# Two pieces of an output projection in the other order: 256 columns ahead of 384

## The chip, the cores and the metric

The kernel runs on one core of one Trainium2 chip. The metric is the device time of one execution in microseconds (us). Three runs of the kernel before took 623.13, 623.89 and 624.4 us. About 0.2%, some 1.25 us, is what a measurement of this kernel can tell from no change.

## The reference, cut to what matters

```python
def _A_ref(x, wqkv, wo):                     # x: 1 x 2048 x 640, H = 32 heads of 20
    qkv = (x @ wqkv).reshape(B, S, 3, H, Dh)...
    # each position attends to W = 8 positions, 2 apart, itself the first
    logits = einsum("bhsd,bhswd->bhsw", q, kg) * scale
    attn = softmax(where(mask, logits, -1e9))
    o = einsum("bhsw,bhswd->bhsd", attn, vg)
    return o.reshape(B, S, D) @ wo

def _B_ref(x, w1, w2):                       # w1: 640 x 1536, w2: 1536 x 640
    return silu(x @ w1) @ w2

xn = layernorm(x)
return x + _A_ref(xn, A_wqkv, A_wo) * silu(_B_ref(xn, B_w1, B_w2))
```

The change concerns the product with `wo`, the output projection of the attention, 640 columns wide.

## The kernel before, in words

The 2048 tokens are worked on in four groups of 512, a group being four tiles (`t`) of 128 tokens. All matrix products are done with 32-bit operands that are split into a high and a low part; a product is the sum of three: high x high, high x low and low x high. The stationary operand of a matmul has 128 x 128 elements, and each matmul has a weight load of its own, also when the stationary operand is the one that is loaded already.

For each group the matmul engine (PE) does, in this order: QKV in four quarters (lines 726 to 760, the matmuls are lines 745 to 747; the first three quarters have 512 columns, the fourth 384); the output projection of the group before (`wo_phase`, lines 796 to 821; not in the first group); and the feed-forward network, FFN, in six stages (`ffn_phase`, lines 877 to 944). A stage of the FFN is two times 15 matmuls of 512 columns (`up`, lines 890 to 892) and then 24 pairs of the kind below (`down`). After the last group comes the output projection of that group (`wo_last`, lines 823 to 875). So three output projections stand between a QKV and an FFN, and a fourth at the end.

The projection and the second product of the FFN have 640 result columns for a token tile, and a PSUM bank holds 512 values. So each product is done as a pair (`tm_mm`, line 770): a 384-column matmul (`CA`, line 774) into a bank of its own for each token tile (`a[t]`), and a 256-column one (`CB`, line 776) into a bank that two token tiles share (`b[t // 2]`). In `wo_phase` the loop runs over the five chunks `c` of 128 of the 640 rows of `wo`. For each chunk the four tiles come one after the other with the high part of the attention's result (`OH`), first times the high, then times the low part of the weights (`big`, four matmuls); then the four tiles with the low part (`OL`) times the high part of the weights (`small`, two matmuls). That is 5 x (4 x 2 + 4) = 60 pairs in a phase, 180 in the three phases. `OH` and `OL` lie in the same tiles (`thl`) that hold the transposed input of QKV, 16 columns further on.

The order of the work is set by a planner (`Weave`, line 63): each step is put on record with its engine, an estimated duration and the buffers that it reads and writes; the steps of PE keep the order in which they are recorded, and those of the other engines are placed by a list scheduler. The matmuls inside `big` or `small` are one step, so their order is that in which the function issues them.

Around `wo_phase`: QKV's last quarter leaves its results in four banks, which ScalarE copies out (lines 533 and 536); these become the four wide banks `a`. The narrow banks `b` are taken first (`tm_banks(True)`) and are two banks of the third quarter. When the projection is finished, VectorE multiplies it by the gate (line 813), the four wide banks first and then the two narrow ones. The FFN writes these banks again in its first `down`, after two `up` steps. The weights come through a ring of seven slots (`w`), filled by DMAs on GpSimd's queue (line 410) as slots are given back (`w_done`).

Of the kernel before, what the change touches and what calls it, by code (L numbers as in the profile page):

```python
# [18 lines left out]
DC, FC = D // P, F // P  # L19
# [35 lines left out]
def tsl(t):  # L55
    return slice(t * P, (t + 1) * P)
# [6 lines left out]
class Weave:  # L63
# [22 lines left out]
    def add(self, eng, dur, fn, reads=(), writes=(), prio=0.0, lock=False, table=None, nbytes=0, late=0.0):  # L86
        o = Op()
        o.late = late
        o.eng, o.dur, o.fn, o.prio, o.lock, o.table, o.nbytes = eng, dur, fn, prio, lock, table, nbytes
        o.seq, o.users, o.ready = len(self.ops), [], 0.0  # L90
        before = set()
        for k in reads:
            if k in self.writer:
                before.add(self.writer[k])
        for k in writes:
            if k in self.writer:
                before.add(self.writer[k])
            before.update(self.readers.get(k, ()))
        for k in writes:
            self.writer[k] = o  # L100
            self.readers[k] = []
        for k in reads:
            self.readers.setdefault(k, []).append(o)
        before.discard(o)
        o.left = len(before)
        for b in before:
            b.users.append(o)
        self.ops.append(o)
        return o
# [104 lines left out]
def local_attention_silu_ffn(ctx: ExitStack, tc: tile.TileContext, x, wqkv, wo, w1, w2, out):  # L214
# [14 lines left out]
    def rows(view, g):  # L229
        h, par = groups[g]  # L230
        return view[h, :, par::2, :]
# [20 lines left out]
    def turned_tiles(half, shift):  # L252
        n = DC * TOK
        return [t[:, half * n + shift:(half + 1) * n + shift].rearrange("p (c m) -> p c m", c=DC) for t in THL]
    TH, TL = turned_tiles(0, 0), turned_tiles(1, 0)
    OH, OL = turned_tiles(0, SHIFT), turned_tiles(1, SHIFT)
# [20 lines left out]
    def take(kind, n):  # L277
        i = count[kind] % n
        count[kind] += 1
        return i  # L280
# [15 lines left out]
    def dve(n, fn, reads, writes, prio, lock=False):  # L296
        add("DVE", dv(n), fn, reads, writes, prio, lock)
# [4 lines left out]
    def pe(dur, fn, reads, writes):  # L302
        add("PE", dur, fn, reads, writes)
        clock[0] += dur

    def dma(fn, reads, writes, nbytes, prio, dur=0.45, late=0.0):
        add("SP", dur, fn, reads, writes, prio, nbytes=nbytes, late=late)
# [125 lines left out]
    def w_next(*want):  # L433

        i = used[0]
        assert units[i] == want and i < loaded[0], (units[i], want)
        used[0] += 1
        s, n = i % RING, width(want)
        return WR[s][:, :n], WR[s][:, n:2 * n], ("wh", s), ("wl", s)

    def w_done(n=1):
        for _ in range(n):
            w_load()
# [318 lines left out]
    def t_keys(i, cs, ts=range(T), kinds=("th", "tl")):  # L762
        return [(k, i, c, t) for k in kinds for c in cs for t in ts]

    def tm_banks(narrow_first=False):
        b = [bank() for t in range(T // 2)] if narrow_first else None
        a = [bank() for t in range(T)]
        return a, b or [bank() for t in range(T // 2)]

    def tm_mm(banks, t, st, w, first, last, cols=(0, 1)):  # L770
        a, b = banks
        h = t % 2
        if 0 in cols:
            nc.tensor.matmul(a[t][0][:, :CA], st, w[:, :CA], start=first, stop=last)  # L774
        if 1 in cols:
            nc.tensor.matmul(b[t // 2][0][:, h * CB:(h + 1) * CB], st, w[:, CA:], start=first and h == 0,  # L776
                             stop=last, skip_group_check=True)

    def tm_views(banks, order="aaaabb"):

        a, b = banks
        n = {"a": 0, "b": 0}
        for kind in order:
            k = n[kind]
            n[kind] += 1
            if kind == "a":
                yield a[k][0][:, :CA].rearrange("p (t m) -> p t m", t=1), a[k][1], slice(k, k + 1), slice(0, CA)
            else:
                yield b[k][0].rearrange("p (t m) -> p t m", t=2), b[k][1], slice(2 * k, 2 * k + 2), slice(CA, D)

    def gkeys(ts, cs):
        return [("g", t, cs.start) for t in range(ts.start, ts.stop)]
# [3 lines left out]
    def wo_phase(g, i):  # L796
        banks = tm_banks(True)
        a, b = banks
        for c in range(DC):
            wh, wl, kh, kl = w_next("wo", c)  # L800
            for t in range(T):
                def big(c=c, t=t, wh=wh, wl=wl):
                    tm_mm(banks, t, OH[i][:, c, tsl(t)], wh, c == 0, False)
                    tm_mm(banks, t, OH[i][:, c, tsl(t)], wl, False, False)
                pe(2 * TM, big, t_keys(i, [c], [t], ["th"]) + [kh, kl], [a[t][1], b[t // 2][1]])
            for t in range(T):
                def small(c=c, t=t, wh=wh):
                    tm_mm(banks, t, OL[i][:, c, tsl(t)], wh, False, c == DC - 1)
                pe(TM, small, t_keys(i, [c], [t], ["tl"]) + [kh], [a[t][1], b[t // 2][1]])
            w_done()  # L810
        for p, kp, ts, cs in tm_views(banks):
            n = (ts.stop - ts.start) * (cs.stop - cs.start)
            dve(n, lambda p=p, ts=ts, cs=cs: nc.vector.tensor_tensor(
                out=G[:, ts, cs], in0=p, in1=G[:, ts, cs], op=OP.mult), [kp], gkeys(ts, cs), 0)
        for t in range(T):
            s = take("xr", 2)
            xr = XR[s]
            dma(lambda t=t, xr=xr: nc.sync.dma_start(xr, rows(xg, g)[:, t, :]), [], [("xr", s)], P * D * 4, clock[0] + 5)
            add("POOL", po(D), lambda t=t, xr=xr: nc.gpsimd.tensor_tensor(out=xr, in0=xr, in1=G[:, t, :], op=OP.add),
                [("g", t, 0), ("g", t, CA)], [("xr", s)], 500, lock=True)  # L820
            dma(lambda t=t, xr=xr: nc.sync.dma_start(rows(og, g)[:, t, :], xr), [("xr", s)], [], P * D * 4, clock[0] + 20)
# [165 lines left out]
```

## Time and profile before

| | |
|---|---|
| median of three runs | 623.89 us (623.13 to 624.4) |
| the profiled execution | 621.75 us, its span 620.0 us |
| instructions | 9090 |
| PE: matmuls | 3357, busy 614.5 us |
| three output projections between QKV and FFN | from 195.06, 346.88 and 498.56 us, 18.00, 18.00 and 17.99 us each |
| output projection at the end | from 598.95 us |
| DMA | 162.45 MB, mean 262 GB/s |

The time of an execution is longer than its span by 1.75 us, which lie around the first and the last instruction. In the views, PE is the matmul engine and PEld its weight loads, which overlap the matmuls. A matmul's duration in the trace is modelled and overlaps the next one's, so a matmul's cost is read from the distance between two starts. `L774` is line 774 of the kernel. In a row of the form `acc<-w,thl` the output stands left of the arrow (`acc` and `rot` are PSUM banks), the operands right of it. In the timeline the first number is the start in microseconds from the start of the span, the second the duration; what stands in brackets at the end of a row is the idle time of the engine before it and what ended that.

### The profile page before, as it was taken

What the parts mean: (1) busy time and instruction counts of PE and PEld (TensorE: products, weight loads), DVE (VectorE), ACT (ScalarE), POOL (GpSimd) and SP (SyncE); (2) the same over time, 40 slices, a digit from 0 to 9 for tenths busy, and PEclk for the clock granted to TensorE, in tenths of its full rate; (3) what the DMA queues carried; (4) which work ended last, traced back from release to release, by engine and by line L of the source; (5) the groups of instructions that cost most, each with busy time, mean ns of one, the idle gap of its engine ahead of it and who ended that gap; (6) DMA issues with size and microseconds to landing.
All of it is one profiled execution on the core that took longest, in us unless ns stands there. A gap on an engine that the chain in (4) does not pass through costs nothing.

```text
span 620.0 us, 9090 instructions
## 1 busy us (share of the span) xinstructions
PE 614.5 (99%) x3357; PEld 555.1 (90%) x3357; DVE 562.0 (91%) x581; ACT 309.5 (50%) x651; POOL 112.9 (18%) x168
## 2 busy tenths in 40 slices
PE   8999999999999999999999999999999999999997
PEld 7889899998889999999888999999988999999997
DVE  6458999999989998999999989999979999899974
ACT  5435558927476213951944502583396316153650
POOL 4510000001101133111212233311121213311100
PEclk9999999999999999999999999999999999999999
DMA  8999999876999998764799999855579999966642
GB/s 255 339 277 321 358 369 395 333 236 174 349 299 350 341 347 247 239 194 136 204 240 255 338 327 309 270 179 162 167 198 277 253 328 277 318 184 194 206 135 102
DMA packets 65449, 162.45 MB, mean 262 GB/s; under 512 B 7053, under 2 KB 29165, under 8 KB 65405
## 3 DMA queue, kind: packets, MB, share of 16 engines
q0 software_dynamic: 20016, 82.58, 44.5%
q1 hardware_dynamic: 45389, 79.29, 40.4%
q8 instruction: 26, 0.43, 0.3%
q14 instruction: 18, 0.15, 0.1%
HBM read 109.55 MB, written 34.16 MB: 232 GB/s over the span
## 4 chain that ended last, share of the span: by engine, by line
PE 97%; SPq 1%; DMA 1%; DVE 0%; issue 0%; ACT 0%
PE acc L774 22%; PE acc L776 15%; PE acc L747 10%; PE acc L746 10%; PE acc L745 10%; PE rot L892 9%; PE rot L891 9%; PE rot L890 9%; PE acc L684 1%; DMA xin<-in_A_x_dram 1%; PE rot L776 1%; SPq L384 0%; SPq L385 0%; PE rot L774 0%; PE acc L872 0%; PE rot L662 0%
## 5 line engine op out<-in xcount | busy, mean ns | idle before, releaser
L747 PE MATMUL acc<-w,thl 128*128 128x512 f32 (+1 forms) x300 | 112.5, 375 | 0.0
L746 PE MATMUL acc<-w,thl 128*128 128x512 f32 (+1 forms) x300 | 112.5, 375 | 0.0
L745 PE MATMUL acc<-w,thl 128*128 128x512 f32 (+1 forms) x300 | 112.5, 375 | 0.0
L774 PE MATMUL acc<-w,sh 128*128 128x384 f32 x384 | 111.6, 334 | 0.0
L776 PE MATMUL acc<-w,sh 128*128 128x256 f32 x384 | 107.3, 279 | 0.0
L896 ACT ACTIVATE sh<-rot 128x512 fp32r<-128x512 f32 x48 | 28.7, 597 | 155.4 <-PE rot L892 155.4
L892 PE MATMUL rot<-thl,w 128*128 128x512 f32 x240 | 93.9, 391 | 0.0
L891 PE MATMUL rot<-thl,w 128*128 128x512 f32 x240 | 93.8, 391 | 0.0
L890 PE MATMUL rot<-thl,w 128*128 128x512 f32 x240 | 93.6, 390 | 0.0
L579 DVE TENSOR_TENSOR pr<-q,kv 128x2560 f32<-128x2560 f32 x32 | 90.1, 2817 | 1.5 <-DMA raw<-in_A_wqkv_dram 1.3
L617 DVE TENSOR_TENSOR pr<-e,kv 128x2560 f32<-128x2560 f32 x32 | 90.3, 2822 | 0.7
L582 DVE TENSOR_REDUCE l<-pr 128x128 f32<-128x2560 f32 x32 | 90.0, 2813 | 0.5
L622 DVE TENSOR_TENSOR pr<-pr 128x1280 f32<-128x1280 f32 x64 | 74.0, 1156 | 1.5
L410 POOL DMA_DIRECT2D w<-half_w x72 | 38.5, 535 | 191.8 <-PE acc L776 98.5
L776 PEld LDWEIGHTS acc<-w,sh 128*128 128x128 f32 x384 | 72.3, 188 | 0.9
L774 PEld LDWEIGHTS acc<-w,sh 128*128 128x128 f32 x384 | 72.1, 188 | 1.1
L410 POOL DMA_DIRECT2D w<-half_q x52 | 27.6, 531 | 238.6 <-PE rot L892 107.2
L774 PE MATMUL acc<-w,thl 128*128 128x384 f32 x225 | 65.5, 341 | 0.0
L745 PEld LDWEIGHTS acc<-w,thl 128*128 128x128 f32 x300 | 56.3, 188 | 8.7
L746 PEld LDWEIGHTS acc<-w,thl 128*128 128x128 f32 x300 | 56.3, 188 | 8.7
L747 PEld LDWEIGHTS acc<-w,thl 128*128 128x128 f32 x300 | 56.3, 188 | 8.5
L495 ACT ACTIVATE xin<-sf 32x256 f32<-32x256 f32 (+1 forms) x144 | 54.6, 379 | 9.7 <-DVE sf L522 8.0
(92 smaller groups left out, 1044.7 us busy)
## 6 DMA issues: line engine op xcount, KB each, us to landing
w<-half_w POOLq DMA_DIRECT2D x72, 640.0 KB, 5.8
w<-half_q POOLq DMA_DIRECT2D x39, 512.0 KB, 4.5
half_w<-w SPq DMA_DIRECT2D x24, 640.0 KB
w<-half_wo POOLq DMA_DIRECT2D x15, 640.0 KB, 5.5
kv<-kv SPq DMA_DIRECT2D x15, 560.0 KB
half_q<-w SPq DMA_DIRECT2D x15, 512.0 KB
kv<-kv SPq DMA_DIRECT2D x15, 420.0 KB
gate<-in_B_w_dram SPq DMA_DIRECT2D x16, 320.0 KB
```

Of the source, the lines that this page charges most:

```text
L579: dve(2560, lambda t=t: nc.vector.tensor_tensor(out=PR, in0=win(qq[:, t:t + 2, :], W, 0), in1=win(kv[:, 0, t:t + 2, :], W, CQ), op=OP.mult ...
L582: dve(2560, lambda t=t: nc.vector.tensor_reduce(out=l[:, t:t + 2].rearrange("p t w h -> p (t w h)"), in_=PR.rearrange("p t w (h d) -> p (t ...
L617: dve(2560, lambda t=t, v=v: nc.vector.tensor_tensor(out=PR.rearrange("p t w (h d) -> p t (w h) d", d=DH), in0=e[:, t:t + 2].rearrange("p ...
L622: dve(2 * k * CQ, lambda k=k: nc.vector.tensor_tensor(out=PR[:, :, 0:k, :], in0=PR[:, :, 0:k, :], in1=PR[:, :, k:2 * k, :], op=OP.add), [] ...
L745: nc.tensor.matmul(o, hi, wh, start=c == 0, stop=False)
L746: nc.tensor.matmul(o, lo, wh, start=False, stop=False)
L747: nc.tensor.matmul(o, hi, wl, start=False, stop=c == DC - 1)
L774: nc.tensor.matmul(a[t][0][:, :CA], st, w[:, :CA], start=first, stop=last)
L776: nc.tensor.matmul(b[t // 2][0][:, h * CB:(h + 1) * CB], st, w[:, CA:], start=first and h == 0, stop=last, skip_group_check=True)
L890: nc.tensor.matmul(h, wh[:, cs], TH[i][:, c, :], start=c == 0, stop=False)
L891: nc.tensor.matmul(h, wh[:, cs], TL[i][:, c, :], start=False, stop=False)
L892: nc.tensor.matmul(h, wl[:, cs], TH[i][:, c, :], start=False, stop=c == DC - 1)
```

## The change

In `wo_phase` alone the 256-column matmul of each pair is issued ahead of the 384-column one. `tm_mm` is rewritten so that the argument `cols` gives the order, not only the choice; FFN and `wo_last` keep calling it with the wide one first. The estimated durations of the steps stay, and so does the planner's order on every engine.

```diff
     def tm_mm(banks, t, st, w, first, last, cols=(0, 1)):
         a, b = banks
         h = t % 2
-        if 0 in cols:
+        def wide():
             nc.tensor.matmul(a[t][0][:, :CA], st, w[:, :CA], start=first, stop=last)
-        if 1 in cols:
+
+        def narrow():
             nc.tensor.matmul(b[t // 2][0][:, h * CB:(h + 1) * CB], st, w[:, CA:], start=first and h == 0,
                              stop=last, skip_group_check=True)
+        for k in cols:
+            (wide, narrow)[k]()
...
                 def big(c=c, t=t, wh=wh, wl=wl):
-                    tm_mm(banks, t, OH[i][:, c, tsl(t)], wh, c == 0, False)
-                    tm_mm(banks, t, OH[i][:, c, tsl(t)], wl, False, False)
+                    tm_mm(banks, t, OH[i][:, c, tsl(t)], wh, c == 0, False, (1, 0))
+                    tm_mm(banks, t, OH[i][:, c, tsl(t)], wl, False, False, (1, 0))
...
                 def small(c=c, t=t, wh=wh):
-                    tm_mm(banks, t, OL[i][:, c, tsl(t)], wh, False, c == DC - 1)
+                    tm_mm(banks, t, OL[i][:, c, tsl(t)], wh, False, c == DC - 1, (1, 0))
```

On PE, the entry of the first output projection, with the last matmul of QKV ahead of it, before. `acc_109` and `acc_110` are wide banks, `acc_107` is the narrow bank of the tiles 0 and 1; behind a row stands the engine on whose work it waits.

```order
L747 MATMUL acc_106<-w_74,thl_71 128x384
L774 MATMUL acc_109<-w_75,thl_67 128x384 [waits Activation_49]
L776 MATMUL acc_107<-w_75,thl_67 128x256
L774 MATMUL acc_109<-w_75,thl_67 128x384 [waits DVE_49]
L776 MATMUL acc_107<-w_75,thl_67 128x256
L774 MATMUL acc_110<-w_75,thl_67 128x384 [waits Activation_49]
```

The same place after the change (the narrow matmul is now line 777):

```order
L747 MATMUL acc_106<-w_74,thl_71 128x384
L777 MATMUL acc_107<-w_75,thl_67 128x256 [waits Activation_49]
L774 MATMUL acc_109<-w_75,thl_67 128x384 [waits Activation_49]
L777 MATMUL acc_107<-w_75,thl_67 128x256 [waits DVE_49]
L774 MATMUL acc_109<-w_75,thl_67 128x384
L777 MATMUL acc_107<-w_75,thl_67 128x256
L774 MATMUL acc_110<-w_75,thl_67 128x384 [waits Activation_49]
```

The narrow matmul has moved up one place in each pair, and the waits for the operands have moved to it; the waits for the wide banks stay with the wide matmuls.

On PE, the end of the same phase and the first matmul of the FFN, before:

```order
L774 MATMUL acc_105<-w_79,thl_67 128x384
L776 MATMUL acc_108<-w_79,thl_67 128x256
L774 MATMUL acc_106<-w_79,thl_67 128x384
L776 MATMUL acc_108<-w_79,thl_67 128x256
L890 MATMUL rot_111<-thl_71,w_80 128x512 [waits DMASW4_49]
```

And after:

```order
L777 MATMUL acc_108<-w_79,thl_67 128x256
L774 MATMUL acc_105<-w_79,thl_67 128x384
L777 MATMUL acc_108<-w_79,thl_67 128x256
L774 MATMUL acc_106<-w_79,thl_67 128x384
L893 MATMUL rot_111<-thl_71,w_80 128x512 [waits DMASW4_49]
```

The phase now ends with a wide matmul. VectorE's, ScalarE's, GpSimd's and SyncE's instructions stand in the same order as before; the one difference there is that VectorE's last product of a phase, the one that reads `acc_108` in the first phase, has lost its wait on PE, since the product of the fourth wide bank ahead of it waits for a later matmul.

## The prediction

> **What bounds the kernel now.** I read the page first, then the waits of PE, then the starts of single matmuls. The page's busy shares, its clock row and its chain of waits by engine:
>
> ```profile
> PE 614.5 (99%) x3357; PEld 555.1 (90%) x3357; DVE 562.0 (91%) x581; ACT 309.5 (50%) x651; POOL 112.9 (18%) x168
> PEclk9999999999999999999999999999999999999999
> PE 97%; SPq 1%; DMA 1%; DVE 0%; issue 0%; ACT 0%
> ```
>
> The matmul engine makes up 97% of the chain, at the full clock. A busy PE need not be a PE at its best pace, though, because matmuls overlap. The view of waits, for PE, has two rows:
>
> ```profile
> PE rot L635 <- POOL ident masks.py:199: 1.4, 1, 1.4
> PE acc L684 <- DVE thl L670: 0.2, 1, 0.2
> ```
>
> Both belong to the first quarter of the first token group. After that PE waits for nobody, so the span is the sum of the distances from one matmul's start to the next, and a change that only reorders matmuls can act only through these distances. The next view is the list of PE's instructions in order of time (start, modelled duration), at the entry and at the end of the first output projection. W stands below for a 384-column matmul (L774), N for a 256-column one (L776):
>
> ```profile
> 194.89 0.34 PE L747 MATMUL acc<-w,thl 128*128 128x384 f32 x1
> 195.06 0.34 PE L774 MATMUL acc<-w,thl 128*128 128x384 f32 x1
> 195.24 0.28 PE L776 MATMUL acc<-w,thl 128*128 128x256 f32 x1
> 195.36 0.34 PE L774 MATMUL acc<-w,thl 128*128 128x384 f32 x1
> ...
> 212.94 0.28 PE L776 MATMUL acc<-w,thl 128*128 128x256 f32 x1
> 213.06 0.40 PE L890 MATMUL rot<-thl,w 128*128 128x512 f32 x1
> ```
>
> From the first W (195.06) to the first matmul of the FFN (213.06) are 60 pairs in 18.00 us: 300.0 ns a pair, 0.18 us after each W and 0.12 us after each N. Now the same pairs, W and N of equal size, elsewhere: in the second half of a stage of the FFN, and in the output projection of the last token group.
>
> ```profile
> 219.87 0.34 PE L774 MATMUL acc<-w,sh 128*128 128x384 f32 x1
> 220.74 0.33 PE L774 MATMUL acc<-w,sh 128*128 128x384 f32 x1
> ...
> 226.76 0.40 PE L890 MATMUL rot<-thl,w 128*128 128x512 f32 x1
> ...
> 233.61 0.34 PE L774 MATMUL acc<-w,sh 128*128 128x384 f32 x1
> ...
> 598.84 0.28 PE L776 MATMUL acc<-w,sl 128*128 128x256 f32 x1
> 598.95 0.33 PE L774 MATMUL rot<-w,thl 128*128 128x384 f32 x1
> ...
> 611.85 2.76 PE L774 MATMUL acc<-w,thl 128*128 128x384 f32 x15
> 614.45 1.87 PE L872 MATMUL acc<-w,thl 128*128 128x256 f32 x15
> ```
>
> In the FFN three pairs take 0.87 us (219.87 to 220.74, 290 ns each), and then 21 pairs take 6.02 us up to 226.76: 286.7 ns. In the last projection 45 pairs go from 598.95 to 611.85 in 12.90 us: 286.7 ns again. The last two rows split a pair: 15 W alone take 614.45 - 611.85 = 2.60 us, 173.3 ns each; of 15 N alone the last ends 1.87 us after the first starts, and with 0.28 us for the last one's own duration that is 1.59/14 = 113.6 ns each. Together 286.9 ns. So 286.7 is what the two members need on their own, and the three projections between QKV and FFN pay 13.3 ns more per pair, without a wait. I call the two paces the short gait and the long gait.
>
> What makes the gait long? The busy table by stretches (PE, PEld, DVE, ACT, POOL, then the granted clock, the DMA share and GB/s):
>
> ```profile
> 195.06:213.06 18.00, 18.00 (x122) 18.00 (x121) 17.80 (x11) 10.13 (x24) 2.64 (x5) 1.00 1.10 336
> 220.74:226.76 6.02, 6.02 (x44) 6.02 (x43) 5.90 (x9) 0.41 (x1) 0.87 (x2) 1.00 0.87 333
> 346.88:364.88 18.00, 18.00 (x122) 18.00 (x121) 16.21 (x17) 2.46 (x6) 2.64 (x5) 1.00 1.17 355
> 498.56:516.55 17.99, 17.99 (x121) 17.99 (x121) 17.34 (x15) 5.29 (x19) 2.65 (x5) 1.00 1.22 334
> 598.95:611.85 12.90, 12.90 (x92) 12.90 (x91) 5.05 (x10) 4.12 (x9) 0.00 (x0) 1.00 0.28 92
> ```
>
> Not the clock (1.00 everywhere). Not VectorE: it is 98% busy in the FFN stretch with the short gait as well. Not the traffic: 333 GB/s there, 336 here. ScalarE's load swings from 2.46 to 10.13 us over the three phases, and the phases still take 18.00, 18.00 and 17.99. Not the tile of the stationary operand either: the last projection reads the same tiles with the same 16-column shift (`OH`, `OL`). What is left is how a run of pairs is entered. Twice the short gait follows something else than a run of 384-column matmuls: 512-column ones in the FFN (after three pairs), short-gait pairs in the last projection. The long gait follows QKV's last quarter, where a 384-column matmul (L747) meets another (W), in all three phases, and once there it holds for 60 pairs.
>
> **The change part by part.** It adds and removes nothing: each of the 180 pairs has the same two matmuls, two weight loads, banks and operands, now N before W.
>
> *The junction from QKV.* L747, 384 columns wide, is now followed by N; the doubled 384-column step is gone. The trace has one junction of that kind: 614.45 above, where 15 W are followed by N alone, and there the following matmuls run at their own 113.6 ns. That is the nearest row, and it has no excess. The bounds for the pair after the change are 286.7 and 300.0 ns from the rows, and on the far side 313.3, if the excess came twice. I take 286.7, because it is the sum of the members' own times and because the long gait has been seen behind one junction only, the one that goes. With three pairs of transition as in the FFN, a phase takes 0.87 + 57 x 0.2867 = 17.21 us in place of 18.00: 0.79 us less.
>
> *The junction to the FFN.* The phase now ends in W. From 213.06 to 219.87 the first 30 matmuls of the FFN take 6.81 us; after short-gait pairs the same 30 take 6.85 (226.76 to 233.61). I charge the 0.04 us. Left: 0.75 us a phase.
>
> *The first waits.* N into its bank now comes first, and carries the wait on ScalarE that W had. W's own wait, for a bank that ScalarE copies out after QKV, comes 0.12 us later in the order. The last of these copies, and the W that first writes that bank:
>
> ```profile
> 195.60 0.22 ACT L536 ACTIVATE q<-acc 128x64 f32<-128x64 f32 x1
> ...
> 196.86 0.34 PE L774 MATMUL acc<-w,thl 128*128 128x384 f32 x1
> ```
>
> The bank is free at 195.82, 1.04 us before its use; the short gait brings that use forward by 6 x 13.3 ns = 0.08 us and N delays it by 0.12. Cost nothing; without that cover, 0.22 us a phase, the copy itself.
>
> *VectorE's products.* They read the banks in the old order, wide ones first. Rows of the second and third phase and of the first, with the idle time before them, and the first matmul of the FFN that writes a bank again:
>
> ```profile
> 213.42 3.14 DVE L813 TENSOR_TENSOR gate<-acc,gate 128x384 f32<-128x384 f32 x6
> 364.06 3.15 DVE L813 TENSOR_TENSOR gate<-acc,gate 128x384 f32<-128x384 f32 x6 [1.55 <-PE acc L774]
> 515.80 3.15 DVE L813 TENSOR_TENSOR gate<-acc,gate 128x384 f32<-128x384 f32 x6 [0.30 <-PE acc L774]
> ...
> 371.69 0.34 PE L774 MATMUL acc<-w,sh 128*128 128x384 f32 x1
> ```
>
> The first wide bank is finished one N (0.12 us) later within its pair, so VectorE waits 0.12 us longer where it waited (1.55 and 0.30 us), and what stands behind it in its queue, the five other products and then attention, moves by as much. The last product loses its wait of its own and finds its bank done earlier. PE needs the banks again at 371.69; the products end at 364.06 + 3.15 = 367.21. With 4.5 us in hand (3.3 in the first phase, 219.87 against 216.56) this costs PE nothing. Without that cover it would be 0.12 us a phase.
>
> *Weight slots.* A slot is given back after its last pair, whichever member ends it, so the loads on POOL's queue start as before, or up to 0.79 us earlier when the phase is shorter. No wait of PE for a load is in the trace. Cost nothing.
>
> **Sum.** 3 x 0.75 = 2.25 us. The profiled execution took 621.75 us, of which 620.0 are the span and 1.75 lie around it; it would become 619.5. The median of the three runs shown is 623.89, 2.14 above that execution, a difference that the reorder does not touch: 623.89 - 2.25 = 621.6 us, 0.36% less.
>
> A rule of the Trainium skill, beside the row of 300.0 ns, speaks against this: "TensorE: Matmul & The Clock Gate", section "Back-to-back issue gap", gives a matmul's distance to the next by its own columns, N/2.4 + 2.5 ns, with no term for what came before. By it a pair would take an estimated 271.7 ns in either order and the change would do nothing; the trace has 300.0 and 286.7 for the same pair, so history matters here and the rule does not settle the case.
>
> **The rivals.**
>
> *The gait stays long (chance 0.36).* Then the alternation behind QKV decides, not its first member: the weights of the first output matmul are still loaded under L747, and after one matmul N, W, N, W is the old sequence. For it: three phases of three, with very different ScalarE load. Against it: the same alternation at 286.7 in the two other places. Time 623.9 (623.3 to 624.5, about the spread of the runs of before).
>
> *Part of it (0.10).* One or two phases change, or the pairs slip into the short gait only midway: 0.75 to 1.5 us, 622.4 to 623.1. All three phases behaved alike before, hence the small chance.
>
> *Slower: a third, longer gait (0.12).* With N first, its weight load and that of W behind it fall under the narrowest matmul straight away, and the excess comes twice a pair: 313.3 ns, 180 x 13.3 = +2.4 us, 626.3. It decides at the first pair: if W's start follows N's by more than 0.12 us, or the next N follows W by more than 0.18. For it: excesses are possible without any wait. Against it: no row has a pair above 300.
>
> That the order does not change at all can be left out: the list of PE's instructions has it changed.
>
> **How the numbers follow.** Short gait in all three phases: 0.42, at 621.6, its own range 620.9 to 622.3. Two runs of before can differ by 0.2% (623.13 to 624.4), so 0.2%, 1.25 us, is about what a measurement of this kernel can tell from no change. Half of the partial case lies beyond it: faster 0.42 + 0.05 = 0.47, same 0.36 + 0.05 = 0.41, slower 0.12. The range runs from 620.9 to 624.5 and leaves out the third gait and the edges. 621.6 is the likeliest case's time, not a mean.
>
> **What would show it.** Right: pairs of 286.7 ns in the three phases, each near 17.2 us from its first N to the FFN's first matmul, that first stretch of the FFN at 6.85, and the span near 617.8. If the phases still take 18.00, the entry is not what sets the gait; if the products on VectorE wait longer but PE's distances stay, that step was right and idle. A new wait of PE in its list would make the whole sum wrong, and so would pairs that change in the FFN, where the order stays.

## The result, and the profile after

| | before | after |
|---|---|---|
| median, first comparison (4 runs each) | 624.04 us (623.13 to 624.4) | 619.91 us (619.63 to 619.97) |
| ratio after/before, with its 95% interval | | 0.9935 (0.9918 to 0.9952) |
| the profiled execution | 621.75 us | 619.89 us |
| its span | 620.0 us | 618.1 us |

The changed kernel is faster by 0.65%, 4.13 us between the medians, where 2.25 were forecast; 619.91 lies below the forecast range. The two profiled executions are only 1.86 us apart. Both differences are taken apart below. The page of the changed kernel, busy shares and chain of waits by engine:

```profile
PE 612.7 (99%) x3357; PEld 553.6 (90%) x3357; DVE 561.5 (91%) x581; ACT 309.1 (50%) x651; POOL 112.6 (18%) x168
PE 99%; DVE 0%; ACT 0%; issue 0%; POOL 0%; POOLq 0%
```

The waits of PE, whole view (time in us, times, longest):

```profile
PE rot L635 <- POOL ident masks.py:199: 1.4, 1, 1.4
PE acc L684 <- ACT w L418: 0.2, 1, 0.2
```

There are still only the two waits at the start, so the time was gained where the prediction looked for it, in the distances from one matmul's start to the next. The list of PE's instructions in order of time, at the entry of the first output projection (N is now L777, W still L774), at its end, and at the end of the first stretch of the FFN:

```profile
195.16 0.34 PE L747 MATMUL acc<-w,thl 128*128 128x384 f32 x1
195.33 0.28 PE L777 MATMUL acc<-w,thl 128*128 128x256 f32 x1
195.45 0.34 PE L774 MATMUL acc<-w,thl 128*128 128x384 f32 x1
195.63 0.28 PE L777 MATMUL acc<-w,thl 128*128 128x256 f32 x1
195.74 0.33 PE L774 MATMUL acc<-w,thl 128*128 128x384 f32 x1
195.91 0.28 PE L777 MATMUL acc<-w,thl 128*128 128x256 f32 x1
...
212.54 0.39 PE L893 MATMUL rot<-thl,w 128*128 128x512 f32 x1
...
219.37 0.34 PE L774 MATMUL acc<-w,sh 128*128 128x384 f32 x1
```

The first pair takes 195.63 - 195.33 = 0.30 us by these rounded starts, W of it 0.18; the second takes 0.28, W of it 0.17. The short gait is there after one pair. The 60 pairs take 212.54 - 195.33 = 17.21 us, and the FFN's first 30 matmuls 219.37 - 212.54 = 6.83. The busy table by stretches for the three phases (columns as before):

```profile
195.33:212.54 17.21, 17.21 (x122) 17.21 (x121) 17.00 (x11) 10.14 (x24) 2.64 (x5) 1.00 1.09 346
346.55:363.75 17.20, 17.20 (x121) 17.20 (x121) 15.98 (x17) 2.45 (x6) 2.64 (x5) 1.00 1.16 369
497.45:514.65 17.20, 17.20 (x121) 17.20 (x121) 16.86 (x14) 4.55 (x16) 2.65 (x5) 1.00 1.23 339
```

Against 18.00, 18.00 and 17.99 of before they are 0.79, 0.80 and 0.79 shorter: 2.38 us, with the same instructions, the clock at 1.00 and ScalarE's load as uneven as before. What the span does not show of it can be read off too. The first phase starts 0.27 us later than before (195.33 against 195.06), and at 262.93 comes a disturbance that this execution pays more for than the one before did:

```profile
262.93 0.45 PE L774 MATMUL acc<-w,sh 128*128 128x384 f32 x1
...
263.33 0.34 PE L774 MATMUL acc<-w,sh 128*128 128x384 f32 x1
...
267.83 0.40 PE L893 MATMUL rot<-thl,w 128*128 128x512 f32 x1
```

One W ran 0.45 us, and the 15 pairs behind it take 267.83 - 263.33 = 4.50 us, 300.0 ns each: the FFN, whose order was not touched, went into the long gait for the rest of this stretch. From 219.37 to 346.55 the execution takes 127.18 us, before 346.88 - 219.87 = 127.01: 0.17 more. The sum is -2.38 + 3 x 0.02 (the FFN's first stretches) + 0.27 + 0.17 = -1.88; the spans differ by 1.9.

So the shorter phases are worth 2.38 us, close to the forecast, and the rest of the 4.13 us between the medians does not come from them. The four runs of before lie 2.29 us (median) above the profiled execution of before, the four of after lie at theirs (+0.02): 1.86 + 2.29 - 0.02 = 4.13.

### The profile page after: what moved, and what is told of

It reads as the page before. It is cut to its first block, busy times and chain, and to the rows that moved or that the text cites. A ratio compares the mean times of both kernels' runs of the same rounds, so it can differ in the third digit from the quotient of the medians.

```text
span 618.1 us, 9090 instructions
## 1 busy us (share of the span) xinstructions
PE 612.7 (99%) x3357; PEld 553.6 (90%) x3357; DVE 561.5 (91%) x581; ACT 309.1 (50%) x651; POOL 112.6 (18%) x168
## 4 chain that ended last, share of the span: by engine, by line
PE 99%; DVE 0%; ACT 0%; issue 0%; POOL 0%; POOLq 0%
PE acc L774 22%; PE acc L777 15%; PE acc L746 10%; PE acc L745 10%; PE acc L747 10%; PE rot L894 9%; PE rot L895 9%; PE rot L893 9%; PE acc L684 2%; PE rot L635 1%; PE rot L777 1%; PE rot L774 0%; PE rot L662 0%; PE acc L875 0%; ACT w L418 0%
## 5 line engine op out<-in xcount | busy, mean ns | idle before, releaser
L774 PE MATMUL acc<-w,sh 128*128 128x384 f32 x384 | 111.7, 334 | 0.0
L777 PE MATMUL acc<-w,sh 128*128 128x256 f32 x384 | 107.1, 279 | 0.0
L774 PEld LDWEIGHTS acc<-w,sh 128*128 128x128 f32 x384 | 72.1, 188 | 1.1
L777 PEld LDWEIGHTS acc<-w,sh 128*128 128x128 f32 x384 | 72.2, 188 | 0.9
L774 PE MATMUL acc<-w,thl 128*128 128x384 f32 x225 | 63.1, 333 | 0.0
```

## The experiments

Each kernel was compared with the kernel before on the same chip; a ratio stands with its 95% interval; it is worked out from all the runs and need not be the quotient of the medians. Letters in the expectations stand for the theories as each expectation gives them. Two questions were open: what picks the gait, and where the 2.29 us come from.

### Where the 2.29 us come from

**before_again**: the kernel before, word for word, compared with itself.

> The kernel before, once more, to see where its timed runs (624.04 us) lose 2.3 us against its profiled execution (621.75 us). Theory U: the three output projections are entered differently from execution to execution, and in most of them the pairs take 313.3 ns in place of 300.0: phases of 18.8 us, spans of about 622.3 us, 180 x 13.3 ns = 2.4 us above the profiled one. Theory V: the rest lies outside the projections, in the start-up before the first matmul of the first quarter or in the QKV or FFN stages: then the phases stay at 18.00 us in every execution and another stretch is longer by about 2 us.

Measured 622.03 us (12 runs, 621.55 to 625.56) beside 622.2 for before (30 runs, 621.6 to 624.57): 1.0004 (0.9991 to 1.0017). Its profiled execution happened to take 624.11, with a span of 622.4. The waits of PE in it that no view above has:

```profile
...
PE acc L774 <- DVE sl L898: 0.8, 1, 0.8
PE acc L745 <- ACT q L536: 0.6, 1, 0.6
...
```

Two waits of PE are new, 1.4 us in sum. Where they lie, by PE's list:

```profile
53.10 0.44 PE L745 MATMUL acc<-w,thl 128*128 128x384 f32 x1 [0.59 <-ACT q L536]
75.06 0.45 PE L774 MATMUL acc<-w,sl 128*128 128x384 f32 x1 [0.84 <-DVE sl L898]
197.44 0.34 PE L774 MATMUL acc<-w,thl 128*128 128x384 f32 x1
```

The first two rows are in the first token group, in QKV's last quarter and in the FFN's first stage. The third is the start of the first output projection, 2.38 us later than in the execution shown of before (195.06). From there to the end both take 424.9 us (622.4 - 197.44 and 620.0 - 195.06), so all of the extra time lies ahead of the first projection. ScalarE, which makes the high parts of the weights (line 418), waits longest for one kind of load between 20 and 80 us in this execution. First that wait, then the same row in the profile shown of before:

```profile
ACT w L418 <- DMA gate<-in_A_wqkv_dram: 10.5, 2, 5.3
```

```profile
ACT w L418 <- DMA gate<-in_A_wqkv_dram: 5.4, 2, 2.9
```

It waits 10.5 us for QKV weights in two pieces, against 5.4 in two. That PE's waits follow from this is likely, not shown. The three output projections took 17.99, 17.99 and 18.00 us in this execution too, so a longer gait in them (theory U) is not what made it slow. What did lies ahead of them, and an execution has it or has not. Of the runs of before, 8 of 30 lay above 623 us here, 7 of 22 and 12 of 29 in two later comparisons.

**after_again** and **after_third**: the changed kernel, word for word, on two chips.

> The changed kernel once more, beside many runs of the kernel before on one chip. Theory S (the change is worth 2.3 us, and the rest of the first comparison came from waits in the first token group that any of these kernels meets in some executions and not in others): medians 2.3 us apart, ratio 0.996, and runs of the changed kernel above 621 us too. Theory R (the change also takes away those early waits): ratio 0.993 to 0.994 again, no run of the changed kernel above 621 us.

> The changed kernel a third time. So far 9 of 9 executions of it were free of waits in the first token group, against some two thirds of the kernel before. Theory S (those waits hit either kernel): with more executions some of the changed kernel lie above 621 us, and the undisturbed ones stay 2.3 us below the undisturbed ones of before. Theory R (the change takes them away): none above 621 us.

Measured 619.75 us (5 runs, 619.39 to 619.99) against 622.37 (22 runs): 0.9949 (0.9934 to 0.9964). Then 620.21 (12 runs, 619.22 to 622.52) against 622.28 (29 runs, 621.65 to 625.82): 0.9958 (0.994 to 0.9976). In the second of them 5 of 12 runs lay above 621 us, so the theory that the reorder rids the kernel of such time falls. None of the three profiled executions of the changed kernel has a new wait of PE; that of first_wide (below), the changed kernel but for one pair of each phase, has one in the FFN's first stage:

```profile
PE acc L774 <- DVE sl L901: 1.4, 1, 1.4
```

The lowest runs of each kernel, which can hold the fewest such waits, are 621.71 - 619.39 = 2.32 and 621.65 - 619.22 = 2.43 us apart, and the gait accounts for 2.38. In the first comparison all four runs of before lay high and none of after. With 27 high runs in 81 that is a rare draw, or a property of that chip; which, no run settles.

### What picks the gait

The forecast rested on one junction: in all three phases the long gait followed a 384-column matmul that met another one. The first four experiments take that explanation apart.

**first_wide**: the changed kernel, only the first pair of each phase as before (W first), so that the doubled 384 is back and N, W follows from the second pair on.

```diff
-    tm_mm(banks, t, OH[i][:, c, tsl(t)], wh, c == 0, False, (1, 0))
+    tm_mm(banks, t, OH[i][:, c, tsl(t)], wh, c == 0, False, (0, 1) if c + t == 0 else (1, 0))
```

> The changed kernel, but the very first pair of each of the three phases has the 384-column matmul first again, so QKV's last 384-column matmul is followed by another, then come two 256-column ones, then narrow ahead of wide. Theory A (the doubled 384-column step at the entry sets the gait for the whole phase): phases of 18.00 us as before, 300.0 ns a pair, a time near 624. Theory B (who is first inside the pairs decides, whatever the entry): 286.7 ns a pair, phases near 17.2 us, 619.9.

Measured 621.23 us (10 runs, 619.27 to 622.7): 0.9974 (0.996 to 0.9988). The first phase, by PE's list:

```profile
197.14 0.34 PE L774 MATMUL acc<-w,thl 128*128 128x384 f32 x1
197.32 0.41 PE L777 MATMUL acc<-w,thl 128*128 128x256 f32 x2
197.56 0.34 PE L774 MATMUL acc<-w,thl 128*128 128x384 f32 x1
...
214.36 0.39 PE L893 MATMUL rot<-thl,w 128*128 128x512 f32 x1
```

It took 214.36 - 197.14 = 17.22 us, as did the other two, though the doubled 384 is there. So the doubled step does not by itself make the gait long.

**first_narrow**: the reverse, the order of before with only the first pair of each phase turned.

```diff
-    tm_mm(banks, t, OH[i][:, c, tsl(t)], wh, c == 0, False, (1, 0))
+    tm_mm(banks, t, OH[i][:, c, tsl(t)], wh, c == 0, False, (1, 0) if c + t == 0 else (0, 1))
```

(The other two calls of `tm_mm` go back to W, N.)

> The kernel before, but in the very first pair of each phase the 256-column matmul goes first; after it the 384-column ones of the first and the second pair stand next to each other, then wide ahead of narrow. Theory A in its narrow form (what follows QKV's last matmul decides): 286.7 ns a pair, phases near 17.2 us, 619.9. Theory A in its wide form (any two 384-column matmuls in a row bring the long gait): 300.0 ns, 18.00 us, near 624. Theory B (who is first inside the pairs): 300.0 ns, near 624.

Measured 620.53 us (5 runs, 619.8 to 621.94): 0.9974 (0.9961 to 0.9987).

```profile
195.44 0.28 PE L777 MATMUL acc<-w,thl 128*128 128x256 f32 x1
195.56 0.51 PE L774 MATMUL acc<-w,thl 128*128 128x384 f32 x2
195.90 0.28 PE L777 MATMUL acc<-w,thl 128*128 128x256 f32 x1
...
212.65 0.40 PE L893 MATMUL rot<-thl,w 128*128 128x512 f32 x1
```

Again 212.65 - 195.44 = 17.21 us, with 59 of the 60 pairs in the order of before. So it isn't the order inside the pairs either: one turned pair at the entry brings the whole gain of the phase.

**one_phase**: N first in the first of the three phases alone.

```diff
-    tm_mm(banks, t, OH[i][:, c, tsl(t)], wh, c == 0, False, (1, 0))
+    tm_mm(banks, t, OH[i][:, c, tsl(t)], wh, c == 0, False, (1, 0) if g == 0 else (0, 1))
```

(The other two calls likewise.)

> Only the first of the three phases has narrow ahead of wide, the other two as before. If the phases are independent and the whole gain lies in them: the first phase 17.2 us, the others 18.00, and a third of the measured 4.1 us: about 622.7. By the predicted 0.75 us a phase alone: 623.3. If the 1.7 us beyond the prediction come from outside the phases and hang on any one of them: 621 to 622.

Measured 621.26 us (10 runs, 620.81 to 624.18): 0.9988 (0.9974 to 1.0002).

```profile
196.95 0.28 PE L777 MATMUL acc<-w,thl 128*128 128x256 f32 x1
...
214.15 0.39 PE L893 MATMUL rot<-thl,w 128*128 128x512 f32 x1
...
348.00 0.34 PE L774 MATMUL acc<-w,thl 128*128 128x384 f32 x1
...
365.99 0.40 PE L893 MATMUL rot<-thl,w 128*128 128x512 f32 x1
```

17.20 us with N first, 17.99 with W first, in one execution; the third phase took 18.00. Each phase picks for itself. The interval touches 1: a third of the gain is about as much as the medians can tell.

**mid_swap**: the order of before, but in one pair in mid-phase, the high product of the weights' high part at chunk 2, tile 0, N goes first.

```diff
-    tm_mm(banks, t, OH[i][:, c, tsl(t)], wh, c == 0, False, (1, 0))
+    tm_mm(banks, t, OH[i][:, c, tsl(t)], wh, c == 0, False, (1, 0) if (c, t) == (2, 0) else (0, 1))
```

> Wide ahead of narrow as before, but in one pair in the middle of each phase (third chunk, first tile, 25th of 60 pairs) the narrow one goes first. Theory C (the long gait holds only as long as nothing disturbs it, and one doubled member ends it; the short one is where pairs settle): 24 pairs at 300.0 and 36 at 286.7, phases of 17.5 us. If the order inside the pairs or the entry keeps setting the gait: phases of 18.0 us.

Measured 620.83 us (7 runs, 620.39 to 623.17): 0.9976 (0.9962 to 0.999).

```profile
195.46 0.34 PE L774 MATMUL acc<-w,thl 128*128 128x384 f32 x1
...
202.36 0.34 PE L774 MATMUL acc<-w,thl 128*128 128x384 f32 x1
202.54 0.41 PE L777 MATMUL acc<-w,thl 128*128 128x256 f32 x2
202.78 0.51 PE L774 MATMUL acc<-w,thl 128*128 128x384 f32 x2
203.13 0.28 PE L777 MATMUL acc<-w,thl 128*128 128x256 f32 x1
203.25 0.33 PE L774 MATMUL acc<-w,thl 128*128 128x384 f32 x1
...
213.00 0.40 PE L893 MATMUL rot<-thl,w 128*128 128x512 f32 x1
```

From 195.46 to 202.36 are 23 pairs in 6.90 us, 300.0 ns each; the turned pair makes an N, N and a W, W; from 203.25 to 213.00 are 34 pairs in 9.75 us, 286.8 ns. One sequence of instructions, two gaits in one phase, and one disturbed place between them. This is the clearest of the twelve runs: each gait holds itself, and a disturbance can throw the matmuls from one into the other.

**all_narrow**: the changed kernel with N first in the FFN as well (three more calls of `tm_mm` get `(1, 0)`). There the pairs come behind 512-column matmuls and run in the short gait with W first.

> Narrow ahead of wide in the FFN's pairs too, beside the three projections. The FFN's pairs are at 286.7 already, so the gain is small: the three slower pairs at each of 24 entries (290 ns) may become one and a half as in the projections (5 ns each), and the 15 steps after them may cost 20 ns less: at most 0.6 us, 619.3 beside 619.9 in undisturbed runs. If the FFN's pairs fall into the long gait when entered with the narrow one: 24 x 24 x 13.3 ns = 7.7 us slower, near 627.6.

Measured 625.7 us (6 runs, 625.3 to 626.95): 1.0048 (1.0034 to 1.0061), slower.

```profile
81.92 0.28 PE L777 MATMUL acc<-w,sh 128*128 128x256 f32 x1
...
89.09 0.39 PE L893 MATMUL rot<-thl,w 128*128 128x512 f32 x1
```

24 pairs take 7.17 us, 298.8 ns each: N first, the order that brought the short gait behind QKV, brings the long one here. Neither order is the good one. That it depends on what the run of pairs follows is shown by the output projections of before: the same tiles in the same order run long behind QKV and short behind the FFN's pairs. The FFN's pairs differ in their stationary tiles too (`sh` and `sl`), and no run takes the two apart there.

**last_512**: the order of before; the last matmul of QKV's last quarter is made 512 columns wide, and so is the first one into the same bank. Nobody uses the 128 extra columns, and the last unit takes its three products in another order, so that the pairs follow a 512-column matmul as in the FFN. Widths alone, if they decide, would make W first short, as in the FFN.

```diff
+    ends = n < TOK and t == T - 1
+    if ends and c == 0:
+        nc.tensor.matmul(bank, hi, r[:, :TOK], start=True, stop=False)
...
+    if ends and c == DC - 1:
+        nc.tensor.matmul(o, hi, wl, start=False, stop=False)
+        nc.tensor.matmul(bank, lo, r[:, :TOK], start=False, stop=True)
```

> [...] Theory E (the step in width at the entry picks the gait: from 512 to 384 short, from 384 to 384 long): three pairs of 290 and then 286.7 ns, phases of 17.2 us. If something else that is common to the three phases picks it: 18.0 us.

Measured 622.34 us (8 runs, 621.79 to 624.1): 0.9988 (0.9969 to 1.0007).

```profile
195.01 0.39 PE L752 MATMUL acc<-w,thl 128*128 128x512 f32 x1
195.24 0.34 PE L782 MATMUL acc<-w,thl 128*128 128x384 f32 x1
...
213.22 0.40 PE L898 MATMUL rot<-thl,w 128*128 128x512 f32 x1
```

213.22 - 195.24 = 17.98 us: long, though a 512-column matmul stands ahead of W. The width of the last neighbour does not decide by itself.

**odd_run**: the order of before; one matmul of QKV's last quarter is left out, so that the pairs begin one place earlier in the sequence. If every second place counted, the gait would turn.

```diff
-    nc.tensor.matmul(o, lo, wh, start=False, stop=False)
+    if n == TOK or (c, t) != (DC - 1, T - 1):
+        nc.tensor.matmul(o, lo, wh, start=False, stop=False)
```

> The kernel before, wide first, with one matmul of QKV's last quarter left out (the low x high product of the last chunk for the last tile), so that 59 matmuls of 384 columns and not 60 come ahead of the pairs and each wide one of the projection takes the other place in the alternation of weight loads. Theory G (the place of the wide one in that alternation, together with the width ahead, picks the gait): short, phases of 17.2 us. If only the widths ahead of the entry pick it: 18.0 us as before. The work left out is worth 0.17 us a group, 0.7 us in all.

Measured 621.47 us (8 runs, 620.89 to 622.73): 0.9979 (0.9964 to 0.9994).

```profile
196.39 0.34 PE L775 MATMUL acc<-w,thl 128*128 128x384 f32 x1
...
214.39 0.40 PE L891 MATMUL rot<-thl,w 128*128 128x512 f32 x1
```

214.39 - 196.39 = 18.00 us: still long. The matmuls left out, 0.17 us each, account for the small gain; the parity of the place does not pick the gait by itself.

**no_shift_wide** and **no_shift_narrow**: the kernels before and after, each with the stationary tiles `OH`, `OL` without their shift by 16 columns.

```diff
-    OH, OL = turned_tiles(0, SHIFT), turned_tiles(1, SHIFT)
+    OH, OL = turned_tiles(0, 0), turned_tiles(1, 0)
```

> The kernel before with the stationary operands of the projections not shifted by 16 columns against QKV's. Theory D (the long gait starts with the step from QKV's unshifted stationary operands to shifted ones): no such step, phases near 17.2 us in the wide-first order. Theory C alone (any undisturbed entry from 384-column matmuls): 18.0 us. A third pace would say that the shift sets a pace of its own; the last projection, short at 286.7 ns a pair with the shift, would show it too.

> The changed kernel without the shift of 16 columns. Without the shift the wide-first order took 17.60 us a phase, 293.3 ns a pair, in the phases and at the end alike. If without the shift there is a single pace that no entry changes: 17.6 us again, and the order is worth nothing there. If the entry still picks between two: 17.2 us.

Measured 621.91 us (8 runs, 620.99 to 624.86) with W first, 0.9999 (0.9983 to 1.0016), and 621.48 (8 runs, 621.02 to 622.15) with N first, 0.9973 (0.9954 to 0.9992). The first phase and the last projection with W first:

```profile
194.83 0.33 PE L774 MATMUL acc<-w,thl 128*128 128x384 f32 x1
...
212.43 0.40 PE L890 MATMUL rot<-thl,w 128*128 128x512 f32 x1
...
597.79 0.34 PE L774 MATMUL rot<-w,thl 128*128 128x384 f32 x1
...
611.00 0.34 PE L774 MATMUL acc<-w,thl 128*128 128x384 f32 x1
```

The first phase with N first:

```profile
195.45 0.28 PE L777 MATMUL acc<-w,thl 128*128 128x256 f32 x1
...
213.05 0.39 PE L893 MATMUL rot<-thl,w 128*128 128x512 f32 x1
```

17.60 us in both, 293.3 ns a pair, and 13.21/45 = 293.6 ns in the last projection, which had 286.7 before. Without the shift the projections have one mean pace, halfway between the two gaits, whichever member goes first. So in the projections the shift is what lets two gaits exist, and with it the order at the entry gets its price. It is not the only way to them: the FFN's pairs, whose stationary tiles `sh` and `sl` have no such shift, were seen at 286.7, at 298.8 (all_narrow) and at 300.0 ns (behind 262.93). What about the place of a tile counts, no run shows.

## Why the prediction was right or wrong

**The bound: right.** PE makes up 99% of the chain after, and its list of waits still has only the two at the start.

**The two gaits and the junction from QKV: the sum right, the explanation too narrow.** The phases were forecast at 17.21 and took 17.21, 17.20 and 17.20. But "how a run of pairs is entered" was pinned on the doubled 384-column step, and first_wide has that step and the short gait. The entry counts, but as one disturbance among others: a pair turned at the start or in mid-phase does the same. "Not the tile of the stationary operand either" was half right: the last projection showed that the shift does not force the long gait, but in the projections there are two only with the shift. The forecast for a phase came out because the junction after the change happens to lead to the short gait, for a reason other than the one given, and that is luck; the row of 15 N (614.45), on which it leaned, is no evidence for that, as all_narrow shows: there N first led to the long one. The chance of 0.36 for "stays long" was therefore not too high.

**Transition and junction to the FFN: sizes.** One pair of transition instead of three, and 6.83 us in place of 6.81 for the first stretch of the FFN, where 6.85 was forecast. Together some 0.02 us a phase: 2.38 - 0.06 = 2.32 measured for 2.25.

**First waits and weight slots: right.** No wait of PE on ScalarE's copies or on a load came up in the three phases.

**The sign in the FFN.** Pairs that change in the FFN were to make the sum wrong, and one stretch did change: from 260.58 to 267.83 it took 7.25 us, where before had 7.04. It is not the order's doing: after_third, the changed kernel, has 7.04 there, and no_shift_wide, with the old order, 7.25.

**VectorE's products: the cost right, the size wrong.** The second phase's first product after the change, with the idle time before it:

```profile
363.09 1.02 DVE L816 TENSOR_TENSOR gate<-acc,gate 128x384 f32<-128x384 f32 x2 [0.98 <-PE acc L774]
```

It waits 0.98 us, not 1.55 + 0.12: the phase is also 0.80 us shorter, so its bank is done earlier, 1.55 + 0.12 - 0.80 = 0.87 as an estimate. In the third phase the wait of 0.30 us is gone. The step moved the wide bank within its pair and forgot that the same change had shortened the phase. PE felt nothing of it, as forecast.

**The step that failed** is the last one of the sum: "2.14 above that execution, a difference that the reorder does not touch". The reorder indeed does not touch it; but it was no fixed distance between a profiled execution and a run, and it did not carry over. In the later comparisons most runs of before lay near the profiled 621.75 (medians 622.2, 622.37 and 622.28), and the changed kernel was 2.62 and 2.07 us below them between medians, for 2.25 forecast. Four profiled executions lie 1.8 to 2.6 us above the lowest run of their kernel, and all four lost time ahead of the first projection: it starts at 197.44 us in before_again, 197.14 in first_wide, 196.95 in one_phase and 196.39 in odd_run, against 195.06 in the execution shown of before, and each has new waits of PE in the first token group. An execution has these or has not. The four runs of after lie at 619.63 to 619.97, and the profiled one among them has none, so the median fell by 1.86 + 2.27 us. Carried over whole, the 2.14 put the forecast at 621.6 and the range's lower end at 620.9, above every one of those four. The profiled execution, at 621.75 the lowest time on the table, less 2.25 would have given 619.5; the range had to reach down to there.

Two things about it are argued, not shown: that the runs of before in the first comparison lay high for the same reason, since no such run was profiled, and that late QKV weights are behind it. ScalarE's wait for them between 20 and 80 us was 10.5, 10.6 and 9.1 us in before_again, first_wide and odd_run, but 5.0 in one_phase, no more than the 5.4 and 4.9 in the executions shown of before and after.

**The rivals.** "Stays long" is what last_512 and odd_run did under other edits (17.98 and 18.00 us), not what this change did. A third, longer gait did not come; the third pace there is, 293.3 ns, belongs to tiles without the shift. "Part of it" is what a disturbance in mid-phase does (mid_swap, 17.54 us a phase).

The rule that was set beside the rows gives an estimated 271.7 ns for a pair, whatever came before it. The Trainium skill, "TensorE: Matmul & The Clock Gate", section "Back-to-back issue gap", has that formula for an isolated matmul, and says that in a stream of weight loads and matmuls both set the spacing. Here each matmul has a weight load of its own, so the formula was no forecast for these pairs and did not speak against the change. The runs have 286.7, 293.3 and 300.0 ns for a pair, and mid_swap two of them in one phase.

**Open** is what in the matmul engine picks a gait. Shown to be not enough, each by itself: the doubled 384, the order inside the pairs, the width of the last neighbour, the parity of the place; VectorE, traffic and the clock were alike in both gaits. A guess at a hidden state that the entry sets fits all twelve runs, but none of them shows it.

## What to carry to other kernels

Where an engine is busy all the time and waits for nobody, list the distances from start to start: the same pair of instructions at 300.0 ns in one stage and at 286.7 in another can be time to be had by an edit of one line, and the place to try is the entry of the run, in both orders, since the order that helps behind one predecessor costs behind another. When a profiled execution lies below all the runs, find out whether the difference is a fixed distance or waits that come and go before it goes into a forecast; if unknown, both ends belong in the range. And compare the lowest runs of both kernels beside the medians: they told 2.32 and 2.43 us in the two later comparisons, while the three medians told 4.13, 2.62 and 2.07. It takes enough runs, though: with four of each, in the first comparison, the lowest were 623.13 - 619.63 = 3.50 us apart.

## What the runs showed of the hardware that was not expected

- An alternation of 384- and 256-column matmuls, each with its own weight load, has two paces that hold themselves, 286.7 and 300.0 ns a pair, at the full clock and without a wait. One out-of-order pair in mid-phase is enough to go from one to the other (mid_swap).
- In the projections without the 16-column shift of the stationary tiles there is one mean pace, 293.3 ns, in either order.
- A disturbance redraws the pace, and not always alike: the W of 0.45 us at 262.93 left the FFN at 300.0 ns a pair up to the end of that stretch in the profiled execution of the changed kernel. The stretch took 7.25 us there and 7.04 in the profile of after_third, the same kernel.
- Loads of the first QKV weights can keep ScalarE waiting for 10.5 us in one execution and for 5.4 in another of the same kernel, and 27 of 81 executions of before lay above 623 us, where the lowest took 621.6.
